# Twenty-seven row tiles of x transposed and stored during the first threshold search

## The chip, the cores and the metric

The kernel runs on one core of a Trainium2 chip. The metric is the device time of one execution in microseconds (us); several executions are taken and their median is compared. The core has five engines that run their own instruction streams in order: TensorE (PE, with its weight loads shown apart as PEld), VectorE (DVE), ScalarE (ACT), GpSimd (POOL) and SyncE (SP, which here only issues DMAs).

## The reference: what is computed

Three stages follow each other: a causal attention without softmax whose scores decay with distance, a mixture of experts in which tokens are handed out greedily by their logits, and a gated feed-forward over all 4608 tokens.

```python
ret = scale * (q @ k.T) * gamma ** (i - j)          # i >= j, else 0; 8 batches, 8 heads, 576 x 64
x = (ret @ v).transpose(0, 2, 1, 3).reshape(4608, 512)
logits = x @ w_gate                                  # 4608 x 8
for idx in argsort(-logits.flatten()):               # greedy: a token goes to one expert,
    ...                                              # an expert takes at most 576 tokens
out[mask_e] = relu(x[mask_e] @ w1[e]) @ w2[e]        # 8 experts, 512 -> 1024 -> 512
h = out @ w_in
y = (h * sigmoid(1.702 * h)) @ w_out                 # 512 -> 2048 -> 512
```

## The kernel before, in words

**Attention stage.** `build` walks over 40 chunks `n`: 8 batches of 576 tokens, each in four chunks of 128 and one of 64. In the loop at the end of `build`, chunk `n` issues, in program order: the load of chunk `n+5` (`load`, on SP), decays on POOL (`prep`), the score matmuls of the *next* chunk (`qk(n+1)`, L797, whose products DVE scales and masks on L800), a few decode steps of the last stage's weights (`decode_steps`: loads and stores on SP, ACT, DVE and POOL work), one `fill()`, then the outputs of this chunk (`yout(n)`, L814 and L819, evicted by ACT on L823 into `xT`), the state update (`state(n)`, L833, evicted on L836), and a second `fill()`. Every engine keeps this order.

**Fills.** `fill()` takes the first entry of the list `fills`, if there is one, and issues it. Two batches form a group `g` of nine row tiles of 128 tokens; as the tiles of a group are completed in `xT`, entries are appended: `logit1` (L848, the gate's matmul on `xT`), `logit2` (L862, transposes of the logits, with a DVE sum on L864), and `rows(g, t)`. After a group's last `logit2` DVE computes at once the best logit and a one-hot mark per token (`argmax`, L128 to L138) and the comparisons `ind` with 128 candidate thresholds (`above`, L144); the matmuls that count them (L156, `count`) are appended to `fills` as a further entry. In the last group the counts are cut in four parts.

**Rows.** `rows(g, t)` makes four 128x128 transposes on PE (L874) from `xT` into a PSUM tile `pY` (two buffers, shared with `yout`), an ACT copy into `xr` (L876, three buffers) and a 256 KB store of `xr` to the DRAM tensor `xd` on the ACT queue (L878). The gathers of the expert stage (L403, indirect DMA on POOL) read their tokens from `xd`, so they wait for all 36 stores. `GDEF` is the number of row tiles that go into `fills`; the others go into a list `later`.

**First threshold search.** When `fills` is drained, `R.phase(0, True)` searches, for the first expert that fills up, the logit from which on it takes tokens. Level 0 was counted in the attention stage; levels 1 to 5 each do: DVE compares with 32 candidates (L144, in three parts), PE counts (L222, 36 small matmuls), DVE thresholds the counts (L226), PE weighs them (L256), DVE forms the next candidates (L268, L274). Then come prefix sums over tokens (L319, L320 on PE), slot numbers on DVE and POOL (L323 to L345), and matmuls that turn slots into a list of token numbers (L351, L362), copied to `gi` on DVE (L366). `phase` is a generator; at its `yield`s the caller may put other work in between. In the caller, a `yield` of `"pe"` (once in each of levels 1 to 5, ahead of L222) or of a positive number calls `fill()` once; `"dve"` and 0 take steps from a list `work`, which is empty here, because all 18 decodes of this stage are issued during attention. What is left in `later` is issued after the generator ends.

**Expert stage.** `ffn` starts with nine matmuls that only keep PE busy (`warm`, L649), the gathers, the first expert's weight loads (L454, on SP, as soon as the expert's number is known), their splits on ACT and DVE (L469, L471), and transposes of the gathered tokens (`prepare`, L420). After that eight experts and nine blocks of the last stage follow, bound by PE.

Of the kernel before, what the change touches and what calls it, by code (L numbers as in the profile page):

```python
# [34 lines left out]
SL, GW, SW, YW = 1, 8, 2, 1  # L35
LGA = 1
X0, XS, XRB = 0, 2.1, 3
PF, XB, GDEF = 5, 3, 30
WU = (9, 3)
AJ = 0  # L40
RF, LD = 4, 4
# [3 lines left out]
ARG, TRI = (2, 6), 6  # L45
# [42 lines left out]
class Route:  # L88
# [82 lines left out]
    def phase(self, k, started=False):  # L171
        nc, V, rt = self.nc, self.nc.vector, self.rt
        last = k == E - 1
        sl = SL if k == 1 else 0
# [9 lines left out]
        else:  # L184
# [3 lines left out]
            for l in range(6):  # L188
                T = 32 if l else 128
                sc = rt([128, 8], BF, name="sc")  # L190
                if l == 0 and started:
                    V.tensor_tensor(sc, self.lastps[:, :8], self.c0, op=OP.is_ge)
                    w = sc
                elif l == 0:
# [11 lines left out]
                    w = sc  # L206
                    V.tensor_scalar(sc, ps[:, :8], CAP - 0.5, None, op0=OP.is_ge)
                elif started:
# [16 lines left out]
                    w = sc[:T]  # L225
                    V.tensor_scalar(w, ps[:T, :8], CAP - 0.5, None, op0=OP.is_ge)  # L226
                else:
# [21 lines left out]
                    w = sc  # L249
# [64 lines left out]
        ei = rt([128, 1], I32, name="ei", bufs=2)  # L314
        V.tensor_scalar(ei, wm1, -1.0, 8.0, op0=OP.mult, op1=OP.add)
        self.EI[k] = ei
        yield 3 + sl if k < 2 else TRI
        ps = self.pm()
        nc.tensor.matmul(ps[:, :72], self.tri, g72, start=True, stop=False)  # L319
        nc.tensor.matmul(ps[:, :72], self.ones, cs[:, 0:72], start=False, stop=True)  # L320
# [22 lines left out]
        for c0, c1 in parts:  # L343
            w = [128, c1 - c0, 64]
            V.tensor_tensor(ohl[:, c0:c1], ll[:, c0:c1, None].to_broadcast(w), self.it64[:, None, :].to_broadcast(w),  # L345
                            op=OP.is_equal)
            if not started:
                yield 3 + sl
        for c0, c1 in parts:
            for c in range(c0, c1, 2):  # L350
                nc.tensor.matmul(ps[:, :36], ohl[:, c:c + 2].rearrange("p c l -> p (c l)"),  # L351
                                 hv[:, c:c + 2].rearrange("p c a h -> p (c a h)"), start=(c == 0),
                                 stop=(c1 == parts[-1][1] and c + 2 == c1))
        yield 0
        pv = rt([128, 2, 2, 9], F16, name="pv")
        V.tensor_scalar(pv.rearrange("p c a h -> p (c a h)"), ps[:, :36], 8192.0, None, op0=OP.min)
        yield 2 + sl
        ps = self.pm()
        po = ps[:, :5]
        for i in range(8):  # L360
# [351 lines left out]
def build(tc, A, out, dbg=None, stop=None):  # L712
# [11 lines left out]
    with ExitStack() as ac:  # L724
# [168 lines left out]
        def fill():  # L893
            if fills:
                f, a = fills.pop(0)
                f(*a)
# [31 lines left out]
        work = []  # L928
        while extra:
            pair = extra[:2]  # L930
            del extra[:2]
            for fs in zip(*pair):
                work += fs
        steps = len(work)
        y = 0
        R.alt = wide
        for w in R.phase(0, True):
            if w == "dve" or w == 0:
                for _ in range(GD):
                    if work:  # L940
                        work.pop(0)()
            else:
                fill()
            y += 1
        R.alt = None
        while fills:
            fill()
# [54 lines left out]
```

## Time and profile before

| | |
|---|---|
| median of 3 runs | 1540.83 us (1539.99 to 1541.78) |
| the profiled execution's own time | 1543.02 us |
| its span, first to last instruction | 1541.2 us |
| PE busy in the span | 1466.0 us (95%) |
| mean granted TensorE clock | 0.975 of full speed |
| attention stage | from 0 to about 195 us |
| threshold search, to the first gather | about 195 to 219 us |

The profile lists, for each engine, its instructions with start and duration, what each waited for, and the clock that was granted to TensorE as a share of its full 2.4 GHz (0.50 is 1.2 GHz). A chain of waits follows the work that ended last back through time. In a timeline row the first number is the start, the second the time to the end of the merged instructions, then engine, line, operation, and tile written <- tiles read.

### The profile page before, as it was taken

Reading aid. Unit: us, or ns where it says so; the run is one execution under the profiler, and the core shown is the slowest. Engines: PE = TensorE matmul, PEld = TensorE weight load, DVE = VectorE, ACT = ScalarE, POOL = GpSimd, SP = SyncE. Lnnn points to the kernel's source line nnn. Section 1 sums busy time; section 2 is a strip of 40 time slices with the busy share of each in tenths; the row PEclk is TensorE's granted clock in tenths of the full one; section 3 lists DMA queues with packets and bytes.
Section 4 is the critical chain, followed back from the end, with each engine's and each line's share of the span. In section 5 each row is a group of like instructions: output and inputs, shape, how many; then the busy total and the mean of one; then the engine's idle time right before and its main releaser. Section 6 shows DMA issues by size and latency. Waiting matters only on the chain.

```text
span 1541.2 us, 25721 instructions
## 1 busy us (share of the span) xinstructions
PE 1466.0 (95%) x10031; PEld 1250.3 (81%) x10031; DVE 863.9 (56%) x1759; ACT 610.7 (40%) x1205; POOL 714.0 (46%) x596
## 2 busy tenths in 40 slices
PE   7899869898999999999999999999999999999997
PEld 6788749776897789788978987898789888988885
DVE  4686668787655665566556755575547322332321
ACT  3455414443434443343334333433343434344432
POOL 4766514576415541553245334623462545144643
PEclk9999859999999999999999999999999999999998
DMA  8999444443322432243223322332242333232320
GB/s 326 371 365 385 137 155 141 154 157 135 116 72 94 126 97 83 83 126 110 69 97 114 108 81 98 113 110 83 83 125 99 112 110 100 93 98 93 123 96 28
DMA packets 58858, 202.86 MB, mean 132 GB/s; under 512 B 8304, under 2 KB 8688, under 8 KB 54768
## 3 DMA queue, kind: packets, MB, share of 16 engines
q1 hardware_dynamic: 47008, 171.36, 32.7%
q0 software_dynamic: 5824, 18.88, 3.6%
q10 hardware_dynamic: 5904, 10.98, 1.9%
q8 instruction: 79, 1.29, 0.3%
q14 instruction: 43, 0.35, 0.1%
HBM read 173.93 MB, written 27.26 MB: 131 GB/s over the span
## 4 chain that ended last, share of the span: by engine, by line
PE 70%; DVE 16%; issue 6%; POOL 4%; DMA 2%; ACT 2%; SPq 0%; ACTq 0%; POOLq 0%; DVEq 0%
PE ph L517 14%; PE ph L519 14%; PE ph L518 14%; PE po L517 6%; PE po L518 6%; PE po L519 6%; DVE ind L144 3%; DVE wl L504 3%; PE pR L797 2%; PE pY L819 2%; DVE oh L138 2%; POOL gl L597 2%; PE pY L814 2%; POOL wl L504 1%; DMA qkv<-in_qkv_dram 1%
## 5 line engine op out<-in xcount | busy, mean ns | idle before, releaser
L504 POOL TENSOR_TENSOR wl<-raw,wh 128x512 fp32r<-128x512 f32 x204 | 274.6, 1367 | 238.4 <-ACT wh L469 238.3
L597 POOL TENSOR_TENSOR gl<-g,gh 128x512 fp32r<-128x512 f32 x144 | 204.9, 1423 | 375.4 <-ACT gh L595 371.5
L469 ACT ACTIVATE wh<-raw 128x512 fp32r<-128x512 f32 x416 | 237.6, 622 | 5.2 <-DMA raw<-in_w_dram 5.2
L593 DVE TENSOR_TENSOR g<-ph,sg 128x512 f32<-128x512 f32 x144 | 99.1, 689 | 249.7 <-ACT sg L616 246.4
L517 PE MATMUL po<-wh,gl 128*128 128x512 f32 x576 | 234.2, 407 | 0.8 <-POOL gl L597 0.8
L517 PE MATMUL ph<-yh,wl 128*128 128x512 f32 x576 | 232.9, 404 | 0.0
L518 PE MATMUL po<-wl,gh 128*128 128x512 f32 x576 | 228.5, 397 | 0.0
L519 PE MATMUL ph<-yh,wh 128*128 128x512 f32 x576 | 228.3, 396 | 0.0
L519 PE MATMUL po<-wh,gh 128*128 128x512 f32 x576 | 228.2, 396 | 0.0
L518 PE MATMUL ph<-yl,wh 128*128 128x512 f32 x576 | 226.8, 394 | 0.0
L616 ACT ACTIVATE sg<-ph 128x512 f32<-128x512 f32 x144 | 86.0, 597 | 337.3 <-PE ph L519 321.8
L504 DVE TENSOR_TENSOR wl<-raw,wh 128x512 fp32r<-128x512 f32 x208 | 193.5, 970 | 4.5 <-ACT wh L469 4.0
L517 PE MATMUL ph<-xh,wl 128*128 128x288 f32 (+2 forms) x512 | 154.2, 301 | 7.9 <-DVE hTl L561 3.1
L517 PE MATMUL ph<-hTh,wl 128*128 128x288 f32 x512 | 153.7, 300 | 0.0
L518 PE MATMUL ph<-xl,wh 128*128 128x288 f32 (+2 forms) x512 | 151.3, 296 | 0.0
L519 PE MATMUL ph<-xh,wh 128*128 128x288 f32 (+2 forms) x512 | 151.2, 295 | 0.0
L518 PE MATMUL ph<-hTl,wh 128*128 128x288 f32 x512 | 151.0, 295 | 0.0
L519 PE MATMUL ph<-hTh,wh 128*128 128x288 f32 x512 | 150.7, 294 | 0.0
L519 PEld LDWEIGHTS po<-wh,gh 128*128 128x128 f32 x576 | 108.9, 189 | 26.4
L595 ACT ACTIVATE gh<-g 128x512 fp32r<-128x512 f32 x144 | 90.5, 628 | 99.1 <-DVE g L593 98.9
L517 PEld LDWEIGHTS po<-wh,gl 128*128 128x128 f32 x576 | 109.1, 189 | 24.9 <-POOL gl L597 1.3
L519 PEld LDWEIGHTS ph<-yh,wh 128*128 128x128 f32 x576 | 108.8, 189 | 24.7
(173 smaller groups left out, 2491.7 us busy)
## 6 DMA issues: line engine op xcount, KB each, us to landing
raw<-w SPq DMA_DIRECT2D x144, 512.0 KB, 3.3
raw<-in_w_dram SPq DMA_DIRECT2D x64, 512.0 KB, 3.5
qkv<-in_qkv_dram SPq DMA_DIRECT2D x31, 1024.0 KB, 10.6
xd<-xr ACTq DMA_DIRECT2D x36, 256.0 KB, 6.4
draw<-in_wi_dram SPq DMA_DIRECT2D x16, 512.0 KB, 8.7
w<-dq SPq DMA_DIRECT2D x32, 256.0 KB, 2.5
draw<-in_wo_dram SPq DMA_DIRECT2D x16, 512.0 KB, 5.0
qkt<-in_qkt_dram SPq DMA_DIRECT2D x8, 256.0 KB, 8.0
```

The lines of the kernel that those rows point to most:

```text
L138: V.tensor_tensor(oh[:, c0:c1], eq[:, c0:c1], wm[:, c0:c1, None].to_broadcast([128, n, 8]), op=OP.is_equal)
L144: self.nc.vector.tensor_tensor(ind, self.m[:, c0:c1, None].to_broadcast([128, n, T]), cand[:, None, :].to_broadcast([128, n, T]), op=OP.is_ge)
L469: nc.scalar.activation(h[:, a], r[:, a], AF.Copy)
L504: f()
L517: nc.tensor.matmul(ps, al, bh, start=first, stop=False)
L518: nc.tensor.matmul(ps, ah, bl, start=False, stop=False)
L519: nc.tensor.matmul(ps, ah, bh, start=False, stop=last)
L593: nc.vector.tensor_mul(g, ps, sg)
L595: nc.scalar.activation(gh, g, AF.Copy)
L597: nc.gpsimd.tensor_sub(gl, g, gh.bitcast(FT))
L616: nc.scalar.activation(sg, ps, AF.Sigmoid, scale=1.702)
L797: nc.tensor.matmul(p[:w, s, hp, :w], k[s * 64:(s + 1) * 64, hp], q[s * 64:(s + 1) * 64, hp], start=True, stop=True)
```

## The change

`GDEF` goes from 30 to 9, so that the rows of the first group alone are in `fills` and 27 wait in `later`. (Before, six of them already did.) The `yield`s of `phase` in its first use get names, one new `yield` is added ahead of the matmuls on slots (L351), and `NFILL` says how many rows are issued at each: three in each of five levels, two ahead of L319, eight ahead of L351, one ahead of L362. These are 26; the last is issued when the generator has ended.

```diff
-PF, XB, GDEF = 5, 3, 30
+PF, XB, GDEF = 5, 3, 9
+NFILL = {"pe": 3, "prefix": 2, "slots": 8, "rows": 1}
...
-        yield 3 + sl if k < 2 else TRI
+        yield ("prefix" if started else 3 + sl) if k < 2 else TRI
         ps = self.pm()
         nc.tensor.matmul(ps[:, :72], self.tri, g72, start=True, stop=False)
...
+        if started:
+            yield "slots"
         for c0, c1 in parts:
             for c in range(c0, c1, 2):
                 nc.tensor.matmul(ps[:, :36], ohl[:, c:c + 2].rearrange("p c l -> p (c l)"),
...
-        yield 2 + sl
+        yield "rows" if started else 2 + sl
...
-        steps = len(work)
-        y = 0
         R.alt = wide
         for w in R.phase(0, True):
             if w == "dve" or w == 0:
...
             else:
-                fill()
-            y += 1
+                for _ in range(NFILL[w]):
+                    fill()
```

## Rows read from the trace of the kernel before

**Rows 1.** Windows: length, busy PE, PEld, DVE, ACT, POOL, PEclk, DMA, GB/s.
```profile
0.00:165.00 165.00, 145.95 (x2040) 126.25 (x2041) 105.02 (x168) 79.74 (x162) 105.32 (x95) 0.97 0.96 359
195.00:218.00 23.00, 14.84 (x238) 11.54 (x238) 19.47 (x72) 5.17 (x9) 1.92 (x1) 0.50 0.36 135
```
**Rows 2.** Chain of waits in 63 to 195 us, share by line.
```profile
by line: PE pR L797 17.6%; PE pY L819 17.3%; PE pY L814 14.9%; PE pY L874 8.0%; DVE ind L144 6.7%; PE pS L833 6.3%; issue 3.6%; PE pm L848 3.6%; DVE eq L136 2.8%; DVE eq L135 2.6%; PE pm L862 2.5%; DVE dT L693 1.7%; PE pm L156 1.5%; DVE R L
```
**Rows 3.** Timeline of one search level, clock at 0.50.
```profile
200.96 0.16 PE L256 MATMUL pm<-sc,c_wt 32*128 32x8 bf16 x1 [0.24 <-DVE sc L226]
201.05 1.12 PE L874 MATMUL pY<-idn,xT 128*128 128x128 f32 x4
202.20 0.60 ACT L876 ACTIVATE xr<-pY 128x512 f32<-128x512 f32 x1 [2.20 <-PE pY L874]
202.32 1.18 PE L222 MATMUL pR<-oh,ind 128*32 128x8 f16 x36 [0.16 <-DVE ind L144]
```
**Rows 4.** Chain in order of time: where it passes a row's copy on ACT.
```profile
95.96 0.61 ACT xr L876
```
**Rows 5.** Timeline around the count of group 1 (chunk 21).
```profile
104.17 1.06 PE L814 MATMUL pY<-qs,S 128*128 128x128 f32 x8
106.09 0.63 PE L833 MATMUL pS<-qkv,ks 128*64 128x64 f32 x16
109.48 0.38 PE L156 MATMUL pm<-oh,ind 128*128 128x8 f16 x9 [2.76 <-DVE ind L144]
```
**Rows 6.** Timeline around the counts of chunks 31 and 34.
```profile
148.49 1.06 PE L814 MATMUL pY<-qs,S 128*128 128x128 f32 x8
150.40 0.64 PE L833 MATMUL pS<-qkv,ks 128*64 128x64 f32 x16
152.52 0.38 PE L156 MATMUL pm<-oh,ind 128*128 128x8 f16 x9 [1.49 <-DVE ind L144]
...
165.11 1.00 PE L814 MATMUL pY<-qs,S 128*128 128x64 f32 x8
166.05 0.68 PE L819 MATMUL pY<-R,vt 64*64 64x64 f32 x16
168.08 0.24 PE L156 MATMUL pm<-oh,ind 128*128 128x8 f16 x3 [1.35 <-DVE ind L144]
```
**Rows 7.** Timeline of rows in the attention stage, clock at 1.00.
```profile
139.35 0.66 PE L874 MATMUL pY<-idn,xT 128*128 128x128 f32 x4
140.28 0.60 ACT L876 ACTIVATE xr<-pY 128x512 f32<-128x512 f32 x1
141.03 0.66 PE L874 MATMUL pY<-idn,xT 128*128 128x128 f32 x4
```
**Rows 8.** Timeline from the prefix sums to the first gather's landing.
```profile
211.56 0.22 PE L320 MATMUL pR<-cs,ones 128*128 128x72 f16 x1
216.77 0.33 PE L351 MATMUL pm<-hv,ind 128*128 128x36 f16 x5 [0.34 <-DVE ind L345]
217.39 0.36 PE L362 MATMUL pR<-pv,c_zz 128*128 128x5 f16 x8 [0.28 <-DVE pv L356]
218.79 1.42 POOL L403 DMA_INDIRECT xg<-xd,gi  x1 [3.76 <-DMA raw<-in_w_dram]
222.66 0.66 PE L420 MATMUL ph<-idn,xg 128*128 128x128 f32 x4 [0.64 <-DMA xg<-xd,gi]
```
**Rows 9.** Row stores, 185 to 250 us, then 140 to 185: KB, landing.
```profile
xd<-xr ACTq DMA_DIRECT2D x6, 256.0 KB, 2.0
...
xd<-xr ACTq DMA_DIRECT2D x6, 256.0 KB, 5.7
```
**Rows 10.** Chain: the third gather, on which the first expert's matmuls wait.
```profile
222.03 7.42 DMA xg<-xd,gi
```
**Rows 11.** One load of a chunk, and the first matmuls that use it.
```profile
122.00 0.38 SPq L743 DMA_DIRECT2D qkv<-in_qkv_dram  x1
139.93 0.97 PEld L797 LDWEIGHTS pR<-qkv 64*128 64x128 f32 x16 [0.17 <-DMA qkv<-in_qkv_dram]
```

## The prediction

> **What bounds the kernel now.** I read the windows by stage first. In the attention stage PE is busy 146 of 165 us at a granted clock of 0.97, and the DMA engines 96% of the time; in the threshold search PE is busy 14.8 of 23 us at 0.50, that is at 1.2 GHz throughout [rows 1]. By these shares the rows look like a burden in the first stage and nearly free in the second. The chain of waits says whether that holds. From 63 us, where the rows of groups 1 to 3 begin, to 195 us the chain is mostly PE work, and the rows' transposes (L874) are 8.0% of it [rows 2]. In the search it alternates between DVE and PE, and the timeline of a level shows how little room PE has there: the row starts at 201.05, directly behind the weighing matmul, and ends at 202.17; the counts start at 202.32, having waited 0.16 us for DVE [rows 3]. One row fills the gap. Idle time of an engine inside a chain is spare only up to the next wait.
>
> **The change part by part.** Six of the 27 rows were in the search already; 21 leave the attention stage.
>
> *What leaves.* 8.0% of 132 us is 10.6 us on the chain, about 16 of the 21 rows at 0.6 us; the other five ran where PE waited for something else anyway. Once the chain also goes through a row's ACT copy, 0.61 us [rows 4], with its store's issue behind it: 1.0 us. Next late are the same PE matmuls, since nothing else in a chunk's order moves. I take 11.6 us; the bounds are 6 us, if DVE or POOL comes up behind PE, and 21 x 0.66 = 13.9 us [rows 7].
>
> *What moves without being named.* The rows also were spacers in the list of fills. In chunk 21 the list held one row and then the count of group 1. The first `fill()` took the row, `yout(21)` and `state(21)` followed, and the second `fill()` took the count. Without the row, the first `fill()` takes the count, and the outputs and the state of the chunk stand behind it on PE. The count waits for DVE's comparisons. Before, PE used that time for the row, the outputs and the state (104.17 to 106.72) and then still idled 2.76 us until 109.48 [rows 5]; now it idles from the end of `qk(22)`, and 2.55 us of work comes after the count, with the following chunk's matmuls behind it. Chunk 31 loses the same 2.55 us (148.49 to 151.04) and chunk 34, by its row (3, 2), 1.62 us (165.11 to 166.73) [rows 6]. Together 6.7 us. The longer idle can also lengthen the stretches at 0.50 that follow. I take 1 us for that, between 0 (these stretches exist already) and 5 us. The attention stage then gains 11.6 - 6.7 - 1 = 3.9 us.
>
> *The five levels.* The clock is 0.50 here, and I take it to stay. `rows` has two `pY` buffers: the third row waits until ACT has emptied the first. The copy starts 1.15 us after the row and takes 0.60 [rows 3]; PE resumes 0.15 us later, as 140.88 to 141.03 shows [rows 7]. So the third row starts 1.90 us after the first and ends at 3.02, and the counts start at about 3.07 instead of 202.32 - 201.05 = 1.27 us: 1.8 us a level, 9.0 us in five. DVE then is early in each level, and nothing is gained from that. The bound below is the full clock, in the first rival.
>
> *The prefix.* The second row ahead of L319 ends about when DVE has its operands: 0.1 us (0 to 1.1).
>
> *The slots.* Eight rows stand between L320, which ends at 211.78, and the 18 matmuls of L351. In pairs of 1.90 us they need 3 x 1.90 + 0.85 + 1.12 = 7.7 us, to 219.5 on the old time axis; L351 then takes about 1.0 us (five took 0.33) and ends at 220.5 instead of 217.10 [rows 8]: 3.4 us. But `xr` has three buffers, each held until its store has landed: 2.0 us in the quiet search, 5.7 us in loaded stretches [rows 9]. The first expert's weights are loaded just then, so some rows wait. I take 4.5 us, between 3.4 and 8.
>
> *The last two rows.* The one ahead of L362 puts 1.12 us where PE waited 0.28: 0.85 us. The 27th follows L362, which ends at 217.75: transposes 1.12, copy 0.64, issue 0.03, landing 2.0, so the gathers are free 3.8 us after L362, where the first started 1.04 us after it [rows 8]: 2.8 us. If POOL needs a start-up after its last wait, up to the same 1.04 us comes on top; if the stores land in 5.7 us, 3.7 more; if the gathers find emptier queues, the third, which took 7.42 us [rows 10], lands up to 3.6 us sooner, the first one's 3.87 us (218.79 to 222.66) being the measure [rows 8]. I take 2.5 us (-0.8 to 7.5).
>
> On the clock the Trainium skill has a rule that speaks against the change: "TensorE: Matmul & The Clock Gate", Part 4 (PE-mode transpose), says that transposes don't count as PE activity and don't bring the clock up. In the search one row a level and the counts kept PE busy 14.8 of 23 us without lifting it, which agrees but doesn't prove it, since the counts are tiny matmuls. By the rule the levels cost the 9.0 us above; if transposes count, the first rival holds.
>
> **Sum.** -3.9 + 9.0 + 0.1 + 4.5 + 0.85 + 2.5 = +13.0 us. The profiled execution took 1543.0 us (span 1541.2), so it would take 1556.0; the median of the runs lies 2.2 us under it, at 1540.8, which gives 1553.8 us. After the first gather nothing changes.
>
> **The rivals.**
>
> *The clock rises in the search* (not slower). With three rows a level PE would be busy nearly without a gap, and at 2.4 GHz the third row ends at 1.68 + 0.66 = 2.34 us [rows 7], while 36 counts may fall from 1.18 to 0.6 us. A level then costs 0.45 us more than now, five 2.2 us; the slots end at 218.6 (+1.5), the row ahead of L362 costs 0.4, the end gains 1.1 with quick gathers. That is 3.0 us, less 4.9 in attention (the 1 us for the clock goes too): about -2, 1539 us. It decides from a mean clock of some 0.9 between the attention stage and the gathers. For it: much denser PE work. Against it: 0.50 in all of the search before [rows 1], and three rows every 3.4 us at the higher clock leave PE gaps again.
>
> *The stores, not the transposes, held the attention stage.* 21 stores are 5.5 MB, at 359 GB/s [rows 1] 15.3 us; if DMA sets the pace, the stage gains that instead of 3.9 us, and the sum is +1.6: 1542 us. For it: DMA at 96%. Against it: a load issued at 122.00 is used at 139.93, and the wait for it is 0.17 us [rows 11].
>
> *The stores pace the search.* With landings of 5.7 us, three buffers let a row through every 2.1 us: the slots cost 8 us and the end 6.5, 7.5 more than taken: 1561 us. For it: the weight loads start at that time. Against it: stores landed in 2.0 us in the search.
>
> **How the numbers follow.** The forecast gets 0.55; its own range is 1547 to 1560, from the bounds of its terms taken partly together. The clock rising gets 0.20, split 0.10 faster, 0.08 same, 0.02 slower; the DMA case 0.10 (0.03, 0.05, 0.02); the slow stores 0.15, all slower. About 0.2% (3.1 us) is what a measurement of this kernel tells from no change. Faster: 0.10 + 0.03 = 0.13; same: 0.08 + 0.05 = 0.13; slower: 0.55 + 0.15 + 0.04 = 0.74. The range 1539 to 1562 leaves out the faster half of the first two rivals and a little above.
>
> **What would show it.** Right: levels of about 4.6 us instead of 2.8 at a clock of 0.50; L156 of chunks 21, 31 and 34 ahead of `yout` and idle for 4 us or more; the first gather later after L362 by 2 us or more, behind a store. The attention stage ending only some 4 us sooner. Wrong: a clock near 1.00 in the search, an attention stage shorter by 10 us or more, or levels that keep their 2.8 us.

## The result, and the profile after

The changed kernel takes 1561.0 us (median of four runs, 1557.4 to 1562.4), beside 1541.3 us for the kernel before on the same chip: a ratio of 1.0127 (95% interval 1.0112 to 1.0143). The forecast was 1553.8, the rival in which the stores pace the search 1561. The profiled executions took 1560.7 us (span 1559.0) and 1543.0 us (span 1541.2), so 17.8 us of span have to be accounted for; the medians lie 19.7 us apart, since the profiled execution of the kernel before is slower than its median. Seven points in both timelines cut the stretch where they differ; line numbers after the change are one to three higher.

| Stretch | before, us | after, us | difference | predicted |
|---|---|---|---|---|
| start to the first weighing matmul (L256, now L257) | 194.93 | 196.52 | +1.6 | -3.9 |
| five levels, first to last weighing matmul | 14.41 | 18.45 | +4.0 | +9.0 |
| prefix, to the end of L320 (now L321) | 2.44 | 2.42 | 0.0 | +0.1 |
| slots, to the end of L351 (now L354) | 5.3 | 13.8 | +8.5 | +4.5 |
| to the end of L362 (now L365) | 0.65 | 0.66 | 0.0 | +0.85 |
| to the first gather (L403, now L406) | 1.04 | 5.0 | +4.0 | +2.5 |
| to the first expert matmul (L517, now L520) | 11.47 | 11.13 | -0.3 | 0 |
| the rest | 1310.94 | 1310.96 | 0.0 | 0 |

**The attention stage.** Two views say why taking out 21 rows made it no shorter. First the windows, from 63 us to the stage's end: length, then busy PE, PEld, DVE, ACT and POOL with their instructions, PEclk, DMA share, GB/s. The kernel before:

```profile
63.00:194.90 131.90, 118.79 (x1643) 101.59 (x1644) 94.35 (x165) 63.96 (x132) 84.61 (x70) 0.92 0.80 298
```

and after:

```profile
63.00:196.50 133.50, 111.74 (x1559) 95.56 (x1560) 96.99 (x165) 52.10 (x110) 83.83 (x69) 0.89 0.68 248
```

PE's first number fell by 7.1 us, but the stretch less PE's busy time, its idle time, rose from 13.1 to 21.8 us, by 8.7. The difference is the +1.6. And 84 matmuls fewer should have saved more than 7.1 us, if the clock had not fallen from 0.92 to 0.89. The waits from 63 to 195 us (us in total, times, longest) name what the idle time waits for; before, and then after:

```profile
PE pm L156 <- DVE ind L144: 13.0, 7, 2.8
```

```profile
PE pm L157 <- DVE ind L145: 21.9, 6, 7.4
```

The second view leaves out the last count after the change, which waits 1.40 us until 196.08. Nearly all of the idle time is the counts waiting for DVE's comparisons. The timeline around the count of group 1 after the change, to be read against [rows 5]:

```profile
98.24 1.57 DVE L701 SCALAR_TENSOR_TENSOR dq<-draw,dT 128x512 int32<-128x512 int32 x1
98.44 0.55 PE L865 MATMUL pm<-idn,lg 128*128 128x128 f32 x3
99.85 1.38 DVE L706 TENSOR_SCALAR dT<-dq 128x512 int32<-128x512 int32 x1
101.15 0.24 DVE L867 TENSOR_REDUCE L<-pm 128x24 f32<-128x96 f32 x1
104.98 2.42 DVE L145 TENSOR_TENSOR ind<-m,c_pat 128x1152 f16<-128x1152 f32 x1
107.46 0.40 PE L157 MATMUL pm<-oh,ind 128*128 128x8 f16 x9 [7.38 <-DVE ind L145]
107.72 2.06 PE L817 MATMUL pY<-qs,S 128*128 128x128 f32 x8
109.70 1.96 PE L822 MATMUL pY<-R,qkv 128*64 128x128 f32 x16
...
149.89 0.40 PE L157 MATMUL pm<-oh,ind 128*128 128x8 f16 x9 [4.88 <-DVE ind L145]
...
168.01 0.23 PE L157 MATMUL pm<-oh,ind 128*128 128x8 f16 x3 [3.38 <-DVE ind L145]
```

The count now stands ahead of L817 and L822, as predicted, and idles 7.38 us instead of 2.76; of the three counts named, two idle the predicted 4 us or more (7.38 and 4.88), the third 3.38. Two things more are to be seen. The logits' transposes (L865) end at 98.99, but DVE's sum of them (L867) starts at 101.15: DVE is busy with two instructions of a decode (L701, L706). The transposes ran 3.7 us earlier than before (98.44 against 102.11); the count came only 2.0 us earlier (107.46 against 109.48). And after the idle time L817 takes 2.06 us where it took 1.06 [rows 5]: the granted clock is 0.50 from 105 to 111 us. Before, it was 0.50 there from 110 to 113 us only.

**The search.** The levels after, with their rows, and the clock where it changes (windows of 1 us, columns as above):

```profile
196.52 0.17 PE L257 MATMUL pm<-sc,c_wt 128*128 128x8 bf16 x1 [0.26 <-DVE sc L193]
196.55 2.90 PE L877 MATMUL pY<-idn,xT 128*128 128x128 f32 x12
...
204.06 0.16 PE L257 MATMUL pm<-sc,c_wt 32*128 32x8 bf16 x1 [0.24 <-DVE sc L227]
204.15 1.09 PE L877 MATMUL pY<-idn,xT 128*128 128x128 f32 x8
205.50 0.66 PE L877 MATMUL pY<-idn,xT 128*128 128x128 f32 x4 [0.25 <-ACT xr L879]
206.08 1.06 PE L223 MATMUL pR<-oh,ind 128*32 128x8 f16 x36
207.39 0.16 PE L257 MATMUL pm<-sc,c_wt 32*128 32x8 bf16 x1 [0.24 <-DVE sc L227]
208.05 0.60 ACT L879 ACTIVATE xr<-pY 128x512 f32<-128x512 f32 x1 [1.55 <-DMA xd<-xr]
```

```profile
199.00:200.00 1.00, 1.00 (x26) 0.67 (x25) 0.49 (x4) 0.54 (x2) 0.00 (x0) 0.50 0.68 262
200.00:201.00 1.00, 0.76 (x22) 0.66 (x20) 0.22 (x2) 0.33 (x1) 0.00 (x0) 0.87 0.69 262
```

The first level goes at 0.50 and takes 4.2 us; from about 200.3 us the clock is 1.00, and a level such as that from 204.06 takes 3.33 (2.8 before). The next one waits for a store (last line of the first fence) and takes 4.26. The clock falls back to 0.50 between 217 and 218 us, ahead of the slots' rows. In the slots and up to the gather, the timeline shows the copies on ACT waiting for stores, and the matmuls behind them:

```profile
217.20 0.19 PE L321 MATMUL pR<-cs,ones 128*128 128x72 f16 x1 [0.15 <-DVE ei L316]
218.71 1.49 SPq L457 DMA_DIRECT2D raw<-in_w_dram  x3
223.43 0.60 ACT L879 ACTIVATE xr<-pY 128x512 f32<-128x512 f32 x1 [2.50 <-DMA xd<-xr]
226.83 0.60 ACT L879 ACTIVATE xr<-pY 128x512 f32<-128x512 f32 x1 [2.81 <-DMA xd<-xr]
227.49 3.23 PE L877 MATMUL pY<-idn,xT 128*128 128x128 f32 x12 [2.29 <-ACT xr L879]
230.51 0.72 PE L354 MATMUL pm<-hv,ind 128*128 128x36 f16 x18
231.55 0.34 PE L365 MATMUL pR<-pv,c_zz 128*128 128x5 f16 x8
233.80 0.33 ACTq L881 DMA_DIRECT2D xd<-xr  x1
236.91 1.48 POOL L406 DMA_INDIRECT xg<-xd,gi  x1 [16.27 <-DVE wl L474]
```

The gather's wait is put down to DVE's `wl`; what came last is the store of the 27th row, issued at 233.80 and landed 2.1 us later, 1.0 us ahead of the gather. It is not `wl`, which the gather doesn't need: in the kernel before, the gather starts at 218.79 and the first `wl` only at 219.61. The chain in order of time (start, us, what) shows the store for which the copy at 226.83 waits:

```profile
219.86 6.89 DMA xd<-xr
```

It took 6.89 us where stores in the quiet search before took 2.0 [rows 9].

### The profile page after: what moved, and what is told of

It is laid out like the page before. It is cut to its first block, busy times and chain, and to the rows that moved or that the text cites. A ratio compares the mean times of both kernels' runs of the same rounds, so it can differ in the third digit from the quotient of the medians.

```text
span 1559.0 us, 25732 instructions
## 1 busy us (share of the span) xinstructions
PE 1468.6 (94%) x10031; PEld 1252.5 (80%) x10031; DVE 869.7 (56%) x1759; ACT 611.3 (39%) x1205; POOL 713.9 (46%) x596
## 4 chain that ended last, share of the span: by engine, by line
PE 75%; DVE 15%; DMA 3%; issue 3%; ACT 2%; POOL 1%; ACTq 0%; DVEq 0%; POOLq 0%
PE ph L520 15%; PE ph L522 14%; PE ph L521 14%; PE po L520 7%; PE po L521 7%; PE po L522 7%; DVE wl L507 3%; DVE ind L145 3%; PE pY L822 2%; PE pY L817 2%; DVE oh L139 2%; PE pR L800 2%; PE pm L423 1%; DMA xd<-xr 1%; DMA idn<-in_idn_dram 1%
## 5 line engine op out<-in xcount | busy, mean ns | idle before, releaser
L520 PE MATMUL po<-wh,gl 128*128 128x512 f32 x576 | 234.3, 407 | 0.9 <-POOL gl L600 0.9
L520 PE MATMUL ph<-yh,wl 128*128 128x512 f32 x576 | 232.8, 404 | 0.0
L520 PE MATMUL ph<-xh,wl 128*128 128x288 f32 (+2 forms) x512 | 153.6, 300 | 7.9 <-DVE hTl L564 3.2
L520 PE MATMUL ph<-hTh,wl 128*128 128x288 f32 x512 | 153.7, 300 | 0.0
L520 PEld LDWEIGHTS po<-wh,gl 128*128 128x128 f32 x576 | 109.2, 190 | 25.0 <-POOL gl L600 1.3
```

Source lines behind the costliest of these rows:

```text
L520: nc.tensor.matmul(ps, al, bh, start=first, stop=False)
```

## The experiments

Each is compared with the kernel before by runs on the same chip. The theory going in was that of the table: the order of the count cost the attention stage its gain, and the stores made the slots and the end long.

**The places kept.** The changed kernel, with an empty entry in the list of fills where each of the 21 rows was, so that the counts stay behind `yout` and `state`.

```diff
+                    if GDEF <= g * 9 + t < 30:
+                        fills.append((lambda: None, ()))
```

> The changed kernel with an empty entry in the list of fills wherever one of the 21 rows was taken out, so that every count (L157) keeps its old place behind yout and state. Theory (the counts moved ahead of yout, and that is why the attention stage did not gain): L157 of chunks 21, 31 and 34 idles 3 us or less instead of 7.4, 4.9 and 3.4, the first weighing matmul of the search (196.5 us in the changed kernel, 194.9 in the one before) comes at about 189, and the time is 1553 us (1550 to 1557). Rival (DVE is the bound around the counts, the order on PE does not matter): the weighing matmul stays at 195 to 197 and the time at 1560.

1550.3 us, ratio 1.0070 (1.0053 to 1.0087). The first weighing matmul starts at 185.40: 11.1 us sooner than after the change, 9.5 sooner than before it. Its windows, waits and counts:

```profile
63.00:185.40 122.40, 106.89 (x1559) 91.28 (x1560) 98.13 (x165) 52.35 (x111) 87.46 (x70) 0.94 0.74 273
```

```profile
PE pm L157 <- DVE ind L145: 16.2, 6, 4.8
```

```profile
106.53 0.40 PE L157 MATMUL pm<-oh,ind 128*128 128x8 f16 x9 [4.80 <-DVE ind L145]
...
147.27 0.38 PE L157 MATMUL pm<-oh,ind 128*128 128x8 f16 x9 [2.26 <-DVE ind L145]
...
158.43 0.23 PE L157 MATMUL pm<-oh,ind 128*128 128x8 f16 x3
```

The same 1559 matmuls as after the change are busy 4.9 us less (106.89 against 111.74), and idle is 15.5 us instead of 21.8. So the order cost 6.3 us of waiting and, in this pair of traces, 4.9 us of slower matmuls. The expected 3 us or less held at two of the three counts; the first still waits 4.80 us. Against the kernel before, removal alone saves 11.9 us of busy time and gives 2.4 us back as longer waits for DVE.

The same rows behaved otherwise in this kernel's search. The clock stayed at 0.50 for almost four levels of 4.3 us:

```profile
190.00:191.00 1.00, 1.00 (x6) 1.00 (x5) 0.98 (x4) 0.13 (x1) 0.00 (x0) 0.50 0.68 262
200.00:201.00 1.00, 1.00 (x6) 0.71 (x4) 0.76 (x5) 0.54 (x2) 0.00 (x0) 0.50 0.04 16
201.00:202.00 1.00, 1.00 (x34) 0.83 (x33) 0.00 (x0) 0.54 (x2) 0.00 (x0) 0.87 0.64 248
```

**Six copy buffers.** The changed kernel with six `xr` instead of three.

```diff
-X0, XS, XRB = 0, 2.1, 3
+X0, XS, XRB = 0, 2.1, 6
```

> The changed kernel with six buffers xr instead of three. Theory (the eight rows ahead of the slot matmuls wait for buffers that are held until a store lands beside the weight loads): the time from L321 to the end of the slot matmuls falls from 13.8 us to 9 to 11, and the total to 1557 us (1555 to 1559). Rival (the DMA engines are what is full, and the gathers wait for the last store in any case): the slots get shorter, the wait for the gathers gets longer by the same, 1560 to 1561.

1557.5 us, ratio 1.0115 (1.0099 to 1.0132). From L321's end to L354's end it takes 9.4 us instead of 13.8, and one wait on a DMA is left, put down to a weight load:

```profile
224.45 0.60 ACT L879 ACTIVATE xr<-pY 128x512 f32<-128x512 f32 x1 [1.86 <-DMA raw<-in_w_dram]
...
227.07 0.75 PE L354 MATMUL pm<-hv,ind 128*128 128x36 f16 x18
```

So 4.4 of the slots' 8.5 us were the buffers. From L365 to the gather it still takes 4.7 us: the last store is as late with six buffers as with three. The whole time shows less than 4.4 us, since this execution came into the search 1.3 us later (197.86), with the same instructions up to there; the intervals of the two ratios overlap, and the verdict rests on the stretch.

**Rows as ordinary matmuls.** To see whether transposes count for the clock, the rows' transposes as matmuls with the identity.

```diff
-                nc.tensor.transpose(p[:, ct, :], XT[g][:, ct, t * 128:(t + 1) * 128], idn)
+                nc.tensor.matmul(p[:, ct, :], XT[g][:, ct, t * 128:(t + 1) * 128], idn, start=True, stop=True)
```

> The changed kernel with the rows' transposes written as ordinary matmuls with the identity. Theory (transposes lift the clock as matmuls do): the clock rises in the second level and falls before the slots as in the changed kernel, levels of about 3.3 us, 1561 us within 1.5, as long as one such matmul takes as long as a transpose. Rival (transposes count less than matmuls): the clock rises a level earlier or stays up through the slots, and the search is 2 us shorter or more, 1558.

1568.5 us (two runs), ratio 1.0189. Not a clean test: each of these matmuls became two instructions, so three rows are 24 on PE instead of 12, and a level takes 4.3 us even at full clock.

```profile
198.93 4.67 PE L877 MATMUL pY<-idn,xT 128*128 128x128 f32 x24
203.54 1.06 PE L223 MATMUL pR<-oh,ind 128*32 128x8 f16 x36
```

Here the clock rose at about 202.6 us (0.69 in the window from 202, 1.00 in the next), within the first level's rows, and stayed up. After the change it rose within the first level too, with transposes. That speaks against a difference between the two, but with the places kept the same transposes ran for almost four levels at 0.50, so one run can't decide it.

**The kernel before, with later counts.** No row is moved. One empty entry ahead of most counts lets more of a chunk's matmuls go ahead of each, the opposite of what the change did.

```diff
+            if g < 3 and t1 == 9 or g == 3 and t1 <= 6:
+                fills.append((lambda: None, ()))
```

> The kernel before with one empty entry ahead of each count of groups 0 to 2 and of the first two counts of group 3, so that each count goes one fill later; rows as before. Theory (PE idles 2.6, 2.8, 1.5, 1.4 and 2.3 us at these counts only because of their place): the idles fall under 1 us each, fewer stretches at 0.50, 1535 us (1532 to 1539). Rival (the scaled scores of the next chunk stand behind the same DVE work, so PE waits for those instead): 1541 within 1.5.

1534.7 us, ratio 0.9967 (0.9955 to 0.9979); run again, 1534.5 and 0.9959 (0.9945 to 0.9973). The first weighing matmul starts at 187.39, 7.5 us sooner than before.

```profile
63.00:187.40 124.40, 114.32 (x1638) 97.14 (x1637) 96.67 (x165) 63.74 (x132) 87.08 (x70) 0.95 0.84 315
```

```profile
PE pm L156 <- DVE ind L144: 8.4, 7, 2.0
```

```profile
105.44 1.16 PE L797 MATMUL pR<-qkv 64*128 64x128 f32 x16
...
108.40 0.38 PE L156 MATMUL pm<-oh,ind 128*128 128x8 f16 x9 [1.80 <-DVE ind L144]
...
150.22 0.38 PE L156 MATMUL pm<-oh,ind 128*128 128x8 f16 x9 [0.40 <-DVE ind L144]
```

The following chunk's L797 now runs ahead of the count. With all rows still in the stage, idle falls by 3.0 us against the kernel before, and busy time by 4.5 us at a clock of 0.95 instead of 0.92. Of the five counts with an empty entry ahead, two fell under the expected 1 us (0.40 and 0.23); the others wait 1.56 to 1.95. The levels take 14.4 us as before, so the search pays nothing.

The trace of the repeat says how exact such figures are. It starts the search at 183.45, 3.9 us sooner than the first trace of the same kernel: idle time is 9.2 us instead of 10.1, but busy time 111.3 instead of 114.3, at a clock of 0.99 instead of 0.95. Busy times and gains of the attention stage from single traces are thus uncertain by some 3 to 4 us. The counts' waits repeat better: 8.4 and 8.3 us in these two, and 23.3 and 23.0 in the changed kernel and the one with six buffers, which has its order (PE busy 111.7 and 111.2 us). Moving the counts back gains 7.5 and 11.5 us in its two traces, moving the rows away with the places kept 9.5 in its one: no difference can be told.

**Rows out of the slots, then out of the end.** Both have the places kept. The first leaves 8 rows more in the attention stage and none in the slots; the second leaves 2 more there, with none behind the slots either.

```diff
-PF, XB, GDEF = 5, 3, 9
-NFILL = {"pe": 3, "prefix": 2, "slots": 8, "rows": 1}
+PF, XB, GDEF = 5, 3, 17
+NFILL = {"pe": 3, "prefix": 2, "slots": 0, "rows": 1}
...
+PF, XB, GDEF = 5, 3, 19
+NFILL = {"pe": 3, "prefix": 2, "slots": 0, "rows": 0}
```

> e1_places with the eight rows ahead of the slot matmuls back in the attention stage (19 rows in the search, in the levels, the prefix and the last two). Theory (those eight rows cost the search some 8 us there, and about 0.5 us each on the chain of the attention stage): from L321 to the end of the slot matmuls about 5.4 us instead of 12 to 14, the attention stage 4 us longer than in e1_places, 1546 us (1544 to 1549), 7 us over the kernel before. Rival (the gathers wait for the weight loads anyway): the gather comes no sooner against the slots' end, total 1550.

> e5_noslots with the last two rows, the one ahead of L365 and the one after it, back in the attention stage too (17 rows in the search, all ahead of the prefix sums). Theory (the last store holds up the first gather by 4 us): the gather starts 1.0 us after L365 as in the kernel before, 4 us less than e5_noslots, 1 us back in attention: 1543 us (1541 to 1545). Rival (the split of the weights on ACT, behind the row copies, is as late): the gather is sooner but the first expert's matmuls are not, 1546.

The first: 1545.2 us, ratio 1.0031 (1.0016 to 1.0046). Its search starts at 186.64, 1.2 us later than with the places kept, where 4 were expected. The slots are back at 5.3 us, and the gather is still 4.65 us behind L365. The second: 1541.7 us, 1.0010 (0.9999 to 1.0022), with the gather 1.07 us behind L365's end:

```profile
215.01 0.35 PE L365 MATMUL pR<-pv,c_zz 128*128 128x5 f16 x8 [0.29 <-DVE pv L359]
...
216.43 1.41 POOL L406 DMA_INDIRECT xg<-xd,gi  x1 [3.77 <-DMA raw<-in_w_dram]
```

So the slots' 8.5 us belong to their rows, and nearly all of the 4.0 us ahead of the gather to the last two. Of 27 deferred rows 17 are left here; they pay for themselves and no more. In this run the clock rose at about 190 us, within the first level (from 187.19), and fell back at about 200.3.

**Both.** The last kernel with the later counts too (1539.1 us, 0.9993, 0.9983 to 1.0002: 2.6 us less than without them, where 5 were expected), and the same with 12 deferred rows, two a level and two ahead of the prefix sums:

```diff
+PF, XB, GDEF = 5, 3, 24
+NFILL = {"pe": 2, "prefix": 2, "slots": 0, "rows": 0}
```

> e6_notail with the counts one fill later, as in e4_later_count. Theory (the two edits act in different stretches and add up): 5 us less than e6_notail, 1538 us (1536 to 1541), within 2 us of the kernel before and above e4_later_count, since three rows a level cost more than they free. Rival (without rows between them the stage is bound by DVE and the later count gives nothing): 1543.

> e4_later_count with six rows more in the search: two a level and two ahead of the prefix sums, empty entries where they were. Theory (a second row costs a level 0.85 us at 0.50, six rows give back about 0.5 us each): 1.5 us over e4_later_count, 1536 us (1534 to 1538). Rival (the second row lifts the clock, and the search pays nothing): 3 us under e4_later_count, 1531.

The second: 1535.2 us, ratio 0.9970 (0.9960 to 0.9980), the same as the later counts alone. It enters the search at 184.11, between the two traces of those (187.39 and 183.45), and its five levels take 16.7 us where they took 14.4 before. Whatever the six rows free in the attention stage, the whole time shows no gain from it.

**Counts later still.** Two empty entries for groups 0 to 2 in that kernel.

```diff
+                fills.extend([(lambda: None, ())] * (2 if g < 3 else 1))
```

> e8_two with two empty entries instead of one ahead of the counts of groups 0 to 2, so that yout and state of the next chunk come before them too. Theory (what PE still idles at these counts, 1.4 us at the second, is the same wait on DVE, and the next yout needs scores that stand behind it on DVE): the idle moves to L822 and shrinks little, 1535 us within 1.5, as e8_two. Rival (the idles vanish, and with them the stretches at 0.50 after them): 1531 us.

1534.9 us, ratio 0.9962 (0.9952 to 0.9973): no gain. The first line is the wait that came in place of the count's.

```profile
108.82 0.43 PE L822 MATMUL pY<-R,qkv 128*64 128x128 f32 x2 [0.68 <-DVE R L803]
...
110.90 0.38 PE L157 MATMUL pm<-oh,ind 128*128 128x8 f16 x9
```

This count no longer idles, but PE waits for DVE's `R` instead, if for less. That DVE's own chain is next fits the missing gain, but wasn't tested by shortening it.

## Why the prediction was right in direction and wrong in its terms

The forecast's direction held, but 1561.0 lies 1.0 us over its own range (1547 to 1560), and one of its signs of being wrong came up: a clock of 1.00, in four of the five levels. Its terms, one by one:

*The rows leave the attention stage* (11.6 us taken): 9.5 with the order kept. PE's busy time did fall by 11.9 us. The step that was off is "next late are the same PE matmuls, since nothing else in a chunk's order moves": the count comes next, and DVE, with its decode steps, didn't follow. The bound named that case.

*The spacers* (6.7 us): 6.3 us of idle time. This step held in sum. Two of the three counts cost 2.6 us each against the kernel with the places kept, as worked out (2.55); the third waits 3.38 instead of nothing (1.62 worked out), and the next count gives 1.6 us back.

*"The longer idle can also lengthen the stretches at 0.50"* (1 us, bound 5): 4.9 us in one pair of traces, 4.3 with the six buffers' trace in place of the changed kernel's. This term, mis-sized at the near end of its bounds, did most to turn a forecast gain of 3.9 us into a loss of 1.6. The clues were in [rows 1] and [rows 5]: a mean clock of 0.97 up to 165 us, with PE waiting 2.76 us at one count, meant that stretches at 0.50 were already being entered. How much a given idle time adds is not shown: the two traces of the later counts differ by 3.0 us of busy time with nearly the same idle.

*The five levels* (9.0 us, with the clock taken to stay at 0.50): 4.0. The clock rose to 1.00 at the end of the first level. The half of the first rival that speaks of the clock came true in part: the mean clock from 196.5 us to the first gather was 0.78, where the rival wanted some 0.9. Its price for a level at the higher clock (0.45 us) was close, 3.33 against 2.8, by two errors that cancel: the counts fell only to 1.06 us and not to 0.6, and the rows ended at 2.0 us and not at 2.34. With the places kept, where the clock stayed, levels took 4.3 us against 4.6 predicted. Both prices were nearly right; which clock holds was not to be read from the kernel before. The Trainium skill's rule that the prediction weighed ("TensorE: Matmul & The Clock Gate", Part 4, PE-mode transpose: transposes don't count as PE activity) doesn't agree with the trace. After the change PE ran nothing but twelve transposes from 227.49 to 230.5 us and then half a microsecond of L354's small matmuls, and the granted clock, 0.50 up to there, was 1.00 from 231 on:

```profile
229.00:230.00 1.00, 1.00 (x6) 0.66 (x5) 0.00 (x0) 0.55 (x1) 0.00 (x0) 0.50 0.64 248
230.00:231.00 1.00, 1.00 (x20) 0.94 (x19) 0.00 (x0) 0.60 (x1) 0.00 (x0) 0.51 0.63 246
231.00:232.00 1.00, 1.00 (x23) 0.99 (x20) 0.27 (x2) 0.60 (x1) 0.00 (x0) 1.00 0.62 240
```

*The slots* (4.5 us, bound 8): 8.5. Here the third rival was right, in mechanism and price (8 us): stores beside the first expert's weight loads hold the `xr` buffers, and ACT's copies wait 2.50 and 2.81 us. Six buffers took 4.4 us away, and the rows taken out took the rest. The argument against that rival, landings of 2.0 us in the quiet search [rows 9], was taken from a stretch into which the weight loads didn't yet fall.

*The last rows* (0.85 and 2.5 us): 0 and 4.0. At the end that rival was not right: it wanted 6.5 us from slow landings, and the last store landed in 2.1 us, as the forecast took it. What the forecast left out is the 1.0 us from the landing to the gather, which it had only as a bound ("a start-up after its last wait"); and quicker gathers, for which it allowed a gain of up to 3.6 us, gave 0.3.

*The stores held the attention stage* (rival): not so. With 21 stores gone the stage gained 9.5 us, not 15.3, and DVE ended PE's waits; moving counts alone, with all stores in place, gained 7.5 and 11.5 us.

So the sum of 13.0 us was 4.8 short of 17.8: 5.5 too good in attention and 5.5 in the slots and ahead of the gather, less 5.0 too bad in the levels, the small rest in the two zeros and the -0.3. The nearness of the time owes something to errors that cancel. That the third rival named 1561 is luck in the same way: its sum has the forecast's attention stage and levels in it, both wrong, and its price for the end was 2.5 us too high.

Open stays why the same rows lift the clock within the first level in some kernels (after the change, and with 17 deferred rows) and only in the fourth in another. Also open is why DVE's L145 took 2.42 us at 104.98, as it did before the change at 107.00, when the same shape took 1.35 us at 148.49: that was not tried.

## What to carry to other kernels

An entry in a list of fills is also a spacer: when one is taken out, look up what moves up in its place, what that waits for, and which engine stands behind it. Idle time of an engine in a chain is room only up to the next wait, and a wait that grows can cost nearly as much again in the clock of the matmuls behind it (here 6.3 us of waiting came with 4.9 us of slower matmuls). One trace is not enough to price that: two traces of one kernel differed by 3.0 us of busy time. A store that is moved takes its buffers' lifetimes and its readers along: price it by the landings of the busiest transfers that it will meet in the new place, and keep it off the last steps ahead of its reader.

## What was not expected of the hardware

- The clock rose after 3 us of nothing but transposes and half a microsecond of small matmuls (the windows from 229 us above), and with the same PE work in the levels it rose at the end of the first (after the change, at 200.3 us from 196.5) or in the fourth (places kept, at 201.3 us from 185.4).
- Each ordinary fp32 matmul with the identity became two instructions on PE (288 for 144): a level's three rows took 3.00 us for 24 at full clock, while two rows of transposes took 1.09 us for 8.
- One row store took 6.89 us to land, issued when weight loads had just been queued, beside a median of 2.1 us for the 13 row stores between 215 and 240 us.
